# Joining the low bits of double-precision weights: a ScalarE copy for each chunk, and the engines' orders exchanged

## The chip, the core and the metric

The kernel runs on one core of one Trainium2 chip. The metric is the device time in microseconds (us) of one execution; of several executions the median is given. The engines are TensorE (PE in the rows; PEld are its weight loads), VectorE (DVE), ScalarE (ACT), GpSimd (POOL) and SyncE (SP), and the DMA queues are fed by SP, ACT and POOL.

## What is computed

Attention with a window of 32 positions and 32 global tokens for 8 batches and 8 heads, followed by a dense layer pair with a Mish-like activation. Cut to what matters:

```python
s_g  = scale * q_g @ concat(k_g, k_l).T;  out_g = softmax(s_g) @ v_all
s_ll = where(|i - j| <= 32, scale * q_l @ k_l.T, -1e9)
out_l = softmax(concat(scale * q_l @ k_g.T, s_ll)) @ concat(v_g, v_l)
x = concat(out_g, out_l)            # 8 x 544 tokens, 512 wide
h = x @ w_in                        # 512 x 2048
g = h * tanh(log1p(exp(h)))
out = g @ w_out                     # 2048 x 512
```

The attention inputs are float32. `w_in` and `w_out` arrive as float64, 8 MB each, so the kernel reads each weight as two 32-bit words and makes a float32 of them before it can use it.

## The kernel before

**Weights.** The two matrices are cut into 32 chunks of 512 KB, sixteen for each (`k` from 0 to 15 and from 16 to 31). A chunk is 128 partitions of 512 weights. `w_load` brings it into a raw buffer; chunks 0 to 4 are issued from ScalarE's queue, the others from GpSimd's, and GpSimd waits until the buffer is free. From chunk 21 on a load also waits for the statistic of the first matrix (`gate`). Three VectorE operations make float32 of it: `w_bits` (line 630) shifts the high word left by 3; the first of `w_sum` (line 637) joins sign and top exponent bit of the high word, the second (line 639) joins the low word shifted right by 29, which is its three top bits. Then `w_stat` (line 660) sums squares of a chunk by four small matmuls on TensorE, `w_norm` (lines 671 to 680, 546, 547) makes one scale for each matrix, with a reduction over the partitions on GpSimd between, and `w_split` (lines 537, 709, 710, 530, 715) writes the scaled weights as a high and a low float16 half into `W`. Where several engines can do a copy (`[(ACT, ...), (DVE, ...)]`), the planner picks one.

**Attention.** Units of one batch, one pair of heads and one of four tiles of 128 rows. For each: `scores` (line 895, TensorE), `row_max` (line 921, VectorE), `expo` (line 930, ScalarE), then in the first batch `p_cross` (transposes by TensorE, lines 971 and 985, with copies at line 537), later `p_hi`, `p_lo` and a DMA transpose; `pv` (line 1020, TensorE), `x_norm` (lines 1028 to 1030, VectorE) and `x_cross` (lines 996, 1004, 530, 532). `b_max` (lines 744 to 750) and `b_scale` (line 755 and on) find a scale for the values of each batch, `v_hi` and `v_lo` (lines 537, 830, 831, 530) split the values, and `v_move` copies pieces of them by small DMAs into the tile `vc`, which `pv` needs.

**Dense layers.** The tokens run in 17 blocks of 256. `m1_mm` (line 1173) is the first layer's matmul, `m2_mm` (line 1437) the second's; later blocks use sums of blocks (lines 1342 and 1532). The first block needs all four pairs of heads of the first batch and the split first matrix.

**Order.** Each operation is added as a task with its engine, a cost and its dependencies, numbered in the order of the calls of `add`. The planner (`Plan.run`) orders tasks by due times and modelled costs; then a list written by hand, `MOVES`, moves single tasks: `91 P 271` puts task 91 on TensorE (P; V is VectorE, A ScalarE, G GpSimd, S SyncE) right after task 271. Each engine runs its tasks in that fixed order and waits at each for what it needs. A buffer's next load waits for the last reader of the old content.

Of the kernel before, what the change touches and what calls it, by code (L numbers as in the profile page):

```python
# [73 lines left out]

MOVES = [(int(n), e, int(m)) for n, e, m in (x.split() for x in """91 P 271, 92 P 91, 93 P 92, 307 P 95, 284 P 275, 154 P 313, 350 P 154, 318 P 159, 164 P 330, 169 P 422, 174 P 343, 175 P 348, 176 P 358, 177 P 378, 178 P 392, 389 P 397, 398 P 389,
461 P 398, 179 P 421, 180 P 453, 454 P 180, 181 P 454, 450 P 474, 182 P 450, 475 P 182, 510 P 475, 183 P 510, 185 P 468, 557 P 555, 513 P 556, 526 P 558, 573 P 565, 566 P 573, 559
P 594, 664 P 642, 562 P 664, 580 P 562, 665 P 580, 680 P 665, 681 P 680, 703 P 622, 704 P 703, 625 P 629, 645 P 634, 666 P 645, 672 P 651, 652 P 672, 673 P 669, 705 P 673, 745 P
684, 747 P 745, 715 P 690, 716 P 708, 731 P 746, 732 P 748, 757 P 754, 769 P 757, 758 P 769, 818 P 783, 808 P 800, 35 V 18, 36 V 19, 37 V 20, 38 V 22, 232 V 39, 233 V 46, 43 V 233,
47 V 43, 44 V 47, 261 V 50, 262 V 54, 58 V 262, 56 V 62, 282 V 67, 283 V 71, 291 V 283, 296 V 291, 76 V 296, 267 V 81, 72 V 267, 73 V 83, 78 V 87, 292 V 88, 115 V 292, 111 V 115,
112 V 268, 274 V 297, 107 V 327, 101 V 107, 108 V 309, 103 V 322, 298 V 103, 104 V 298, 113 V 104, 380 V 113, 116 V 380, 328 V 116, 117 V 351, 123 V 119, 352 V 329, 127 V 366, 131  # L80
V 127, 373 V 424, 132 V 425, 133 V 135, 129 V 133, 374 V 129, 439 V 374, 381 V 136, 407 V 139, 137 V 407, 387 V 137, 403 V 387, 388 V 144, 370 V 388, 151 V 370, 371 V 151, 413 V
371, 372 V 413, 414 V 372, 418 V 414, 408 V 418, 384 V 408, 385 V 145, 148 V 448, 156 V 383, 157 V 431, 161 V 157, 412 V 161, 419 V 158, 449 V 419, 471 V 449, 149 V 471, 420 V 149,
396 V 466, 434 V 166, 459 V 401, 446 V 459, 163 V 171, 467 V 163, 168 V 172, 429 V 173, 472 V 429, 465 V 472, 529 V 465, 186 V 529, 480 V 186, 511 V 480, 534 V 188, 483 V 189, 457
V 483, 522 V 191, 512 V 478, 193 V 512, 524 V 193, 540 V 524, 535 V 540, 525 V 489, 195 V 525, 444 V 195, 906 V 444, 530 V 906, 536 V 531, 220 V 536, 907 V 220, 908 V 545, 230 V
908, 542 V 230, 260 V 550, 552 V 260, 520 V 560, 583 V 520, 584 V 583, 278 V 561, 910 V 578, 958 V 579, 587 V 585, 590 V 587, 591 V 588, 959 V 648, 649 V 959, 639 V 569, 620 V 639,
960 V 620, 961 V 960, 554 V 961, 786 V 554, 962 V 610, 624 V 962, 1001 V 643, 1002 V 644, 1003 V 1002, 575 V 1003, 1004 V 575, 687 V 1004, 1005 V 687, 1035 V 657, 621 V 1035, 1208
V 658, 688 V 1208, 1036 V 688, 667 V 678, 650 V 667, 631 V 650, 1037 V 631, 632 V 1037, 1209 V 632, 661 V 1209, 636 V 661, 668 V 636, 784 V 682, 637 V 683, 696 V 785, 697 V 810,
728 V 697, 729 V 706, 812 V 729, 654 V 707, 655 V 723, 700 V 655, 675 V 700, 813 V 1039, 676 V 813, 737 V 1062, 815 V 772, 738 V 815, 850 V 773, 1063 V 850, 730 V 1063, 693 V 1064,
694 V 752, 741 V 694, 718 V 741, 719 V 753, 1066 V 767, 768 V 1066, 776 V 1123, 821 V 776, 805 V 1124, 822 V 805, 806 V 1125, 779 V 734, 760 V 735, 761 V 790, 744 V 816, 1127 V
744, 1146 V 1127, 826 V 817, 1147 V 826, 823 V 1147, 787 V 823, 834 V 787, 797 V 834, 1148 V 797, 798 V 876, 802 V 798, 837 V 802, 803 V 864, 844 V 843, 235 A 226, 294 A 286, 295 A  # L90
294, 105 A 304, 317 A 105, 316 A 314, 312 A 316, 325 A 312, 335 A 331, 326 A 335, 355 A 340, 369 A 337, 342 A 438, 345 A 342, 440 A 344, 402 A 440, 360 A 347, 357 A 360, 359 A 349,
416 A 377, 379 A 416, 417 A 382, 451 A 417, 445 A 399, 395 A 445, 400 A 433, 462 A 400, 458 A 462, 427 A 458, 452 A 427, 469 A 452, 428 A 479, 463 A 428, 470 A 464, 477 A 456, 521
A 477, 482 A 521, 518 A 190, 192 A 443, 538 A 192, 539 A 538, 514 A 194, 219 A 514, 515 A 219, 527 A 515, 541 A 544, 528 A 229, 570 A 528, 519 A 259, 551 A 519, 277 A 551, 909 A
563, 279 A 564, 581 A 279, 567 A 582, 568 A 567, 711 A 609, 646 A 626, 656 A 627, 677 A 647, 713 A 677, 630 A 713, 635 A 630, 1038 A 660, 695 A 685, 720 A 686, 849 A 762, 692 A
849, 717 A 692, 740 A 717, 775 A 770, 804 A 771, 733 A 804, 836 A 833, 481 S 436, 523 S 485, 543 S 547, 640 S 593, 712 S 640, 659 S 749, 679 S 659, 714 S 679, 739 S 702, 764 S 739,
807 S 777""".split(","))]
# [1862 lines left out]
```

## Time and profile before

| | |
|---|---|
| median of 3 runs | 873.93 us (872.58 to 873.93) |
| the profiled execution's own time | 873.65 us |
| its span on the core | 871.9 us |
| TensorE busy | 840.7 us, 96% |
| VectorE busy | 747.9 us, 86% |
| ScalarE busy | 645.9 us, 74% |
| GpSimd busy | 169.4 us, 19% |
| mean DMA rate | 127 GB/s; 365, 372 and 358 in the first three of 40 slices |

The span is the time from the first to the last instruction of the program; what lies around it is 1.75 us here. A busy share is an average over the whole span, so the stages have to be looked at one by one. A row of a timeline gives start, time, engine, line, operation, what it writes and reads, how many were merged, and in square brackets the idle time of the engine ahead of it with what ended it.

### The profile page before, as it was taken

The numbers are of one execution on the slowest core, as the hardware profiler recorded it, in microseconds if no ns is written. First come the engines' busy times: TensorE is split into PE (matmuls) and PEld (weight loads), VectorE is DVE, ScalarE is ACT, GpSimd is POOL, SyncE is SP. The second block draws the span as 40 slices with busy tenths as digits, with TensorE's granted clock in tenths as the row PEclk, the third lists the DMA queues.
The fourth block names the chain that finished last, engine by engine and source line by source line (L and its number), as shares of the span: only waits on it lengthen the run. The fifth ranks groups of instructions, "written<-read, shape, count | busy, mean of one in ns | idle before, by whom it ended". The sixth has DMA issues, their size and how long they took to land.

```text
span 871.9 us, 24740 instructions
## 1 busy us (share of the span) xinstructions
PE 840.7 (96%) x9792; PEld 620.8 (71%) x9792; DVE 747.9 (86%) x1989; ACT 645.9 (74%) x1389; POOL 169.4 (19%) x324
## 2 busy tenths in 40 slices
PE   2789999999999999999999999999999999999997
PEld 1458667766675867876777776777777777689996
DVE  6999999668897798999879987998789999986675
ACT  2588988677698778989888877899888755464542
POOL 6220341033026103402330133112311000000000
PEclk9899999999999999999999999999999999999999
DMA  9994476375897976859676775475657541000000
GB/s 365 372 358 92 120 153 115 60 145 101 180 216 124 194 136 131 150 107 183 126 121 104 170 131 101 89 165 121 122 116 118 89 77 38 1 27 14 14 27 25
DMA packets 206885, 111.07 MB, mean 127 GB/s; under 512 B 186992, under 2 KB 191280, under 8 KB 205744
## 3 DMA queue, kind: packets, MB, share of 16 engines
q1 hardware_dynamic: 193952, 86.23, 48.9%
q0 software_dynamic: 11952, 20.37, 8.0%
q10 hardware_dynamic: 864, 2.88, 0.9%
q8 instruction: 77, 1.26, 0.6%
q14 instruction: 40, 0.33, 0.1%
HBM read 49.04 MB, written 8.91 MB: 66 GB/s over the span
## 4 chain that ended last, share of the span: by engine, by line
PE 89%; DVE 6%; DMA 2%; ACT 1%; issue 0%; POOL 0%; DVEq 0%; ACTq 0%
PE o L1437 33%; PE h L1342 25%; PE h L1173 11%; PE s L895 5%; PE U L1020 5%; PE o L1532 5%; PE gu L1124 1%; PE g L1058 1%; DVE W L637 1%; DMA raw<-in_w 1%; DVE W L639 1%; DVE W L630 1%; DMA W<-in_w 1%; DMA pt<-ph 1%; PE hx L1532 1%; DVE vmx L744 1%
## 5 line engine op out<-in xcount | busy, mean ns | idle before, releaser
L1437 PE MATMUL o<-W,G 128*128 128x512 f16 x1344 | 313.2, 379 | 0.0
L1437 PEld LDWEIGHTS <-G 128*128 128x128 f16 x1344 | 124.9, 98 | 128.5 <-issue 2.6
L1342 PEld LDWEIGHTS <-W 128*128 128x128 f16 x2880 | 166.0, 98 | 9.6 <-issue 0.2
L930 ACT ACTIVATE P<-P,nm 128x192 f32<-128x192 f32 (+1 forms) x256 | 117.8, 461 | 38.8 <-DVE nm L921 38.2
L1173 PE MATMUL h<-xh,W 128*128 128x256 f16 x640 | 114.4, 273 | 0.0
L1173 PEld LDWEIGHTS <-W 128*128 128x128 f16 x960 | 91.1, 98 | 16.7 <-issue 3.0
L1342 PE MATMUL h<-xh,W 128*128 128x128 f16 x1056 | 97.0, 219 | 0.0
L1342 PE MATMUL h<-xl,W 128*128 128x128 f16 x528 | 91.1, 219 | 0.0
L1173 PE MATMUL h<-xl,W 128*128 128x256 f16 x320 | 87.2, 272 | 0.0
L1342 PE MATMUL h<-raw,W 128*128 128x128 f16 x1152 | 73.2, 219 | 0.0
L854 POOL DMA_DIRECT2D vc<-vf x81 | 41.3, 512 | 155.6 <-DVE vf L835 110.3
L1020 PEld LDWEIGHTS <-pt 128*128 128x128 f16 (+1 forms) x1424 | 56.1, 98 | 18.9 <-issue 7.7
L895 PE MATMUL s<-qk 64*128 64x224 f16 (+3 forms) x640 | 56.2, 301 | 7.3 <-DMA qk<-in_qk 6.4
L921 DVE CUSTOM_DVE_ANT_0 P<-s,consts,sq 128x192 f32<-128x192 f32 (+1 forms) x128 | 53.0, 429 | 10.3 <-PE s L895 10.3
L537 ACT ACTIVATE ph<-P 128x384 f16<-128x384 f32 (+1 forms) x112 | 58.7, 538 | 3.3 <-DMA pt<-ph 2.6
L854 POOL DMA_DIRECT2D vgg<-vgf x84 | 44.3, 531 | 85.0 <-issue 47.9
L921 DVE CUSTOM_DVE_ANT_0 P<-s,consts 128x192 f32<-128x192 f32 (+1 forms) x128 | 45.5, 369 | 9.0 <-PE s L895 4.4
L1020 PE MATMUL U<-vc,pt 96*128 96x64 f16 (+1 forms) x656 | 52.3, 193 | 0.0
L1020 PE MATMUL U<-vf,pt 128*128 128x64 f16 x720 | 50.7, 194 | 0.7 <-DMA pt<-ph 0.7
L930 ACT ACTIVATION_READ_ACCUMULATOR P<-P,nm 128x1 f32 x256 | 48.1, 188 | 0.0
L530 ACT COPY EE<-h 128x512 f32<-128x512 f32 x47 | 27.2, 579 | 23.4 <-PE h L1342 16.2
L949 DVE SCALAR_TENSOR_TENSOR ph<-P,ph 128x256 f16<-128x256 f32 x112 | 38.5, 353 | 4.1 <-ACT ph L537 3.5
(281 smaller groups left out, 1750.8 us busy)
## 6 DMA issues: line engine op xcount, KB each, us to landing
qk<-in_qk SPq DMA_DIRECT2D x32, 704.0 KB, 5.2
out<-ob SPq DMA_DIRECT2D x33, 256.0 KB, 2.7
vraw<-in_vm SPq DMA_DIRECT2D x8, 1024.0 KB, 5.9
W<-in_w POOLq DMA_DIRECT2D x14, 512.0 KB, 7.5
raw<-in_w POOLq DMA_DIRECT2D x7, 512.0 KB, 7.3
G<-in_w POOLq DMA_DIRECT2D x6, 512.0 KB, 6.8
W<-in_w ACTq DMA_DIRECT2D x5, 512.0 KB, 10.6
pt<-ph SPq DMA_TRANSPOSE x120, 3.6
```

The costliest lines, as they stand in the source:

```text
L530: A.copy(dst, src)
L537: A.activation(out=dst, in_=src, func=AF.Copy, scale=c)
L854: stream(POOL, dma(kib), lambda: G.dma_start(dst(), src()), 512, r=[r], w=[w], new=new, table="dma")
L895: T.matmul(X[s[h]][:, cols(u)], part(b, hp, i)[r, u * 128:(u + 1) * 128], part(b, hp, j)[r, KO + OWN[u]:KO + OWN[u] + WIDTH[u]], start=n = ...
L921: pl.add(DVE, (134 if b >= QF else 77) + 1.03 * w, lambda: V.tensor_tensor_reduce(out=half(P, h, w), in0=X[s][:, cols(t)], in1=mask[:, m0: ...
L930: pl.add(ACT, 460, lambda: A.activation(out=half(P, h, w), in_=half(P, h, w), func=AF.Exp, bias=X[nm], scale=-1.0, accum_out=X[sums][:, t, ...
L949: pl.add(DVE, dve(2 * (z - a)), lambda a=a, z=z, q=q, o=o: V.scalar_tensor_tensor(X[ph][:, q, :, a + o:z + o], p_src(X[P], t)[:, :, a:z], ...
L1020: T.matmul(X[u][:, t, h, :], X[pt][:k, p * 4 + (c * 2 + h if turned(b, t) else h * 2 + c), :], X[vx][:k, t, vl, h * 64:(h + 1) * 64], star ...
L1173: T.matmul(X[h][:, f * TB:(f + 1) * TB], wh(i, wl)[:, off:off + 128], X[x][:, d, o:o + TB], start=(n == 0), stop=(n == 11))
L1342: T.matmul(X[h][:, c:c + 128], form(J + jj, wl)[:, off:off + 128], x(l, d), start=(p in (1, 2, 5) and c == 0 and n == 0), stop=(n == 5), s ...
L1437: T.matmul(X[o], gp(g, blk, i)[:, f, t * 128:(t + 1) * 128], wh(8 + i, wl)[:, f * 512:(f + 1) * 512], start=(turn == 0 and n == 0), stop=( ...
L1532: T.matmul(X[o][:, cols], a_form(a, jj, f), b_form(w, jj, f), start=(fresh and n == 0), stop=(n == 11), skip_group_check=True)
```

## The change

Where a chunk is in `BY_ACT` (all 32 are), `w_sum` adds a ScalarE task and one VectorE task in place of two VectorE tasks. `w_bits` stays ahead of them. The ScalarE task reads the upper halfword of each low word as an unsigned integer, divides it by 256, adds 4336 + 2^-9 and writes it as bf16 into the lower halfword of the high word: rounding to eight bits leaves the three top bits of the low word in the three lowest bits of that halfword. The VectorE task then takes sign, top exponent bit and those three bits from the high word by one mask and joins them. There are as many tasks as before, so the numbers in `MOVES` mean the same steps, but the list is another one: 387 entries in place of 344. The name `VMAX` is replaced by `VSQ`, which is empty, so that the branches that ask for it stay unused, and one lambda becomes a named function.

```diff
-VMAX = 99
+VSQ = ()
+BY_ACT = range(32)
...
-MOVES = [(int(n), e, int(m)) for n, e, m in (x.split() for x in """91 P 271, 92 P 91, 93 P 92, 307 P 95, ...
+MOVES = [(int(n), e, int(m)) for n, e, m in (x.split() for x in """84 P 237, 89 P 239, 90 P 89, 91 P 90, ...
...
+        if k in BY_ACT:
+
+            def w_low():
+                halves = raw(k).bitcast(U16).rearrange("p (f w) -> p f w", w=4)
+                A.activation(out=halves[:, :, 2].bitcast(BF16), in_=halves[:, :, 1], func=AF.Copy, scale=2.0 ** -8, bias=4336 + 2.0 ** -9)
+            pl.add(ACT, act(512), w_low, r=key, w=[rawkey(k)])
+
+            def w_join():
+                V.scalar_tensor_tensor(f(), word(k, 1), -0x3FFFFFF9, f(), ALU.bitwise_and, ALU.bitwise_or)
+            pl.add(DVE, 610, w_join, r=[rawkey(k)], w=key)
+            return
         pl.add(DVE, 610, lambda: V.scalar_tensor_tensor(f(), word(k, 1), -0x40000000, f(), ALU.bitwise_and, ALU.bitwise_or),
                r=[rawkey(k)], w=key)
         pl.add(DVE, 610, lambda: V.scalar_tensor_tensor(f(), word(k, 0), 29, f(), ALU.logical_shift_right, ALU.bitwise_or),
```

The entries of the new list that put copies of the start-up on VectorE which ran on ScalarE before (the list is otherwise left out; the steps are in the order of the entries):

```
23 V 22 (b_split)   201 V 42, 210 V 233, 241 V 40 (v_hi)   240 V 48, 288 V 274, 302 V 298, 331 V 127 (p_cross)
317 V 113, 319 V 384, 342 V 139, 364 V 414 (w_split)   402 V 129 (p_hi)   377 V 364, 379 V 158 (x_cross)
```

## Rows read from the trace of the kernel before

**Rows 1.** The page's 40 equal slices, busy tenths: TensorE, DMA engines.

```profile
PE   2789999999999999999999999999999999999997
...
DMA  9994476375897976859676775475657541000000
```

**Rows 2.** Windows by stage: length; busy us (instructions) by engine; clock, DMA, GB/s.

```profile
core 0: us, PE busy (x) PEld busy (x) DVE busy (x) ACT busy (x) POOL busy (x), PEclk, DMA share, GB/s
...
20.00:31.00 11.00, 10.23 (x50) 5.53 (x50) 10.83 (x31) 8.70 (x23) 3.03 (x5) 1.00 1.03 397
31.00:42.00 11.00, 6.46 (x75) 5.27 (x76) 10.95 (x29) 3.69 (x15) 3.31 (x6) 0.78 1.02 360
42.00:48.70 6.70, 5.64 (x65) 4.50 (x63) 6.43 (x25) 4.30 (x15) 3.23 (x7) 0.85 0.92 307
48.70:70.64 21.94, 20.29 (x153) 11.98 (x152) 21.87 (x66) 19.84 (x55) 2.40 (x5) 1.00 0.94 325
70.64:110.00 39.36, 39.36 (x405) 30.09 (x403) 38.76 (x92) 36.58 (x66) 8.92 (x18) 1.00 0.42 100
110.00:800.00 690.00, 689.28 (x8219) 500.20 (x8218) 599.55 (x1637) 538.34 (x1158) 134.74 (x260) 1.00 0.61 117
```

**Rows 3.** Windows of line 637 alone: length, VectorE's busy us (instructions), clock, DMA.

```profile
6.60:20.00 13.40, 2.65 (x4) 1.00 1.03 416
20.00:42.00 22.00, 7.95 (x12) 0.89 1.02 378
42.00:48.70 6.70, 1.37 (x2) 0.85 0.92 307
48.70:70.64 21.94, 5.40 (x8) 1.00 0.94 325
```

**Rows 4.** The chain that ended last: start, us on the chain, what.

```profile
16.63 1.20 DVE W L637 x2
```

**Rows 5.** Timeline of TensorE, 19 to 40 us.

```profile
19.16 0.61 PE L660 MATMUL ws<-W 128*128 128x128 bf16 x4 [6.67 <-DVE W L639]
19.70 1.76 PE L895 MATMUL s<-qk 64*128 64x192 f32 x8
...
30.88 0.97 PE L895 MATMUL s<-qk 64*128 64x192 f32 x8
...
39.81 0.61 PE L660 MATMUL ws<-W 128*128 128x128 bf16 x4 [3.34 <-DVE W L639]
```

**Rows 6.** ScalarE's groups by form: count, busy us and mean ns, idle before.

```profile
L530 ACT CAST xs<-x 128x512 f16<-128x512 f32 x24 | 14.8, 615 | 4.5 <-DVE x L1030 4.0
...
L537 ACT ACTIVATE G<-EE,c 128x512 f16<-128x512 f32 x17 | 12.1, 718 | 0.2
```

**Rows 7.** Line 630 by itself: min/median/max ns, first and last start.

```profile
L630 DVE TENSOR_SCALAR W<-W x19: 411/422/1029, 6.6 to 67.9; 128x512 int32<-128x512 int32 x19
```

**Rows 8.** Timeline of VectorE, 40 to 48 us.

```profile
40.28 1.28 DVE L639 SCALAR_TENSOR_TENSOR W<-W 128x512 int32<-128x512 int32 x2
...
44.99 0.28 DVE L671 CUSTOM_DVE_ANT_0 wd<-ws,consts 128x128 f32<-128x128 f32 x1
...
47.88 0.16 DVE L547 RECIPROCAL sw<-iw 128x1 f32<-128x1 f32 x1
```

**Rows 9.** Timeline of TensorE's weight loads: the first of the dense layer.

```profile
70.64 1.25 PEld L1173 LDWEIGHTS <-W 128*128 128x128 f16 x12
```

**Rows 10.** The sixteenth chunk: its issue (timeline), and its us to landing (DMAs).

```profile
31.35 0.53 POOL L612 DMA_DIRECT2D W<-in_w  x1 [2.43 <-DVE W L639]
...
W<-in_w POOLq DMA_DIRECT2D x1, 512.0 KB, 4.5
```

**Rows 11.** Windows by stage around 40 us, columns as in rows 2.

```profile
36.00:40.00 4.00, 0.61 (x7) 0.42 (x7) 4.00 (x10) 0.00 (x0) 0.00 (x0) 0.64 1.02 366
40.00:44.00 4.00, 3.90 (x45) 3.63 (x44) 3.85 (x11) 0.57 (x2) 0.00 (x0) 0.50 1.03 319
```

**Rows 12.** The tile `vc`, 30 to 50 us: its DMAs' time to landing.

```profile
DMA to landing us min/median/max: 3.8/5.9/8.4
```

More of the change, by code (lines that the diff above doesn't have):

```diff
@@ L16 @@
 BF16 = mybir.dt.bfloat16
+U16 = mybir.dt.uint16
 AF = mybir.ActivationFunctionType
@@ L95 @@
-849, 717 A 692, 740 A 717, 775 A 770, 804 A 771, 733 A 804, 836 A 833, 481 S 436, 523 S 485, 543 S 547, 640 S 593, 712 S 640, 659 S 749, 679 S 659, 714 S 679, 739 S 702, 764 S 739,
-807 S 777""".split(","))]
+MOVES = [(int(n), e, int(m)) for n, e, m in (x.split() for x in """84 P 237, 89 P 239, 90 P 89, 91 P 90, 281 P 242, 271 P 269, 92 P 271, 93 P 92, 307 P 97, 263 P 234, 100 P 275, 284 P 299, 154 P 301, 310 P 303, 305 P 310, 350 P 313, 330 P 320, 334
+P 159, 422 P 386, 174 P 356, 175 P 174, 353 P 175, 358 P 353, 176 P 363, 447 P 376, 177 P 378, 389 P 177, 397 P 392, 421 P 461, 178 P 421, 426 P 178, 453 P 426, 179 P 453, 454 P
@@ new lines @@
+50, 240 V 48, 262 V 56, 266 V 262, 62 V 266, 282 V 66, 283 V 282, 60 V 283, 267 V 71, 296 V 267, 291 V 76, 292 V 81, 268 V 88, 297 V 268, 274 V 107, 288 V 274, 308 V 288, 309 V
+101, 322 V 109, 327 V 103, 302 V 298, 328 V 323, 104 V 328, 119 V 104, 113 V 119, 317 V 113, 123 V 351, 370 V 352, 384 V 370, 319 V 384, 371 V 117, 121 V 365, 331 V 127, 125 V 331,
+406 V 424, 131 V 425, 381 V 131, 139 V 381, 342 V 139, 373 V 342, 402 V 129, 439 V 402, 374 V 439, 135 V 374, 156 V 137, 385 V 156, 387 V 385, 407 V 387, 147 V 407, 403 V 147, 388
@@ new lines @@
+V 403, 413 V 388, 405 V 413, 372 V 151, 414 V 372, 364 V 414, 377 V 364, 158 V 377, 379 V 158, 418 V 379, 161 V 418, 419 V 161, 141 V 419, 383 V 141, 430 V 383, 412 V 153, 458 V
+412, 149 V 163, 420 V 448, 431 V 449, 396 V 431, 466 V 396, 459 V 466, 463 V 459, 467 V 463, 433 V 467, 166 V 433, 445 V 166, 434 V 445, 462 V 434, 446 V 462, 479 V 446, 171 V 471,
+480 V 171, 511 V 472, 529 V 511, 429 V 168, 400 V 429, 408 V 173, 401 V 408, 534 V 401, 464 V 534, 473 V 464, 465 V 186, 483 V 189, 457 V 483, 478 V 191, 512 V 478, 522 V 512, 193
@@ new lines @@
+V 522, 524 V 193, 535 V 524, 530 V 535, 540 V 530, 525 V 540, 906 V 195, 531 V 500, 536 V 531, 907 V 220, 545 V 907, 908 V 545, 230 V 908, 520 V 560, 583 V 520, 584 V 583, 561 V
+584, 910 V 578, 579 V 910, 585 V 958, 590 V 587, 591 V 588, 959 V 648, 280 V 649, 620 V 280, 569 V 620, 639 V 569, 960 V 639, 961 V 960, 786 V 554, 623 V 786, 962 V 610, 1001 V
+643, 1002 V 644, 1003 V 1002, 575 V 1003, 1004 V 575, 1005 V 687, 1035 V 657, 621 V 1035, 1208 V 658, 688 V 1208, 1036 V 688, 667 V 678, 650 V 667, 1209 V 650, 1037 V 631, 661 V
@@ new lines @@
+632, 636 V 661, 784 V 682, 683 V 784, 785 V 637, 696 V 785, 810 V 696, 811 V 697, 729 V 706, 812 V 729, 654 V 707, 655 V 723, 700 V 655, 675 V 700, 1039 V 724, 813 V 1039, 676 V
+813, 1062 V 676, 737 V 1062, 815 V 772, 738 V 815, 850 V 763, 1063 V 850, 730 V 1063, 1064 V 730, 693 V 1064, 694 V 752, 741 V 694, 1066 V 767, 1123 V 768, 776 V 1123, 1124 V 821,
+805 V 1124, 1125 V 822, 806 V 1125, 734 V 774, 735 V 779, 761 V 790, 744 V 816, 1127 V 744, 1146 V 1127, 826 V 817, 1147 V 826, 823 V 1147, 787 V 823, 834 V 787, 797 V 834, 1148 V
@@ new lines @@
+797, 798 V 876, 802 V 798, 837 V 802, 24 A 36, 250 A 203, 14 A 250, 47 A 226, 51 A 238, 228 A 51, 243 A 228, 63 A 55, 236 A 264, 270 A 59, 286 A 77, 252 A 286, 295 A 87, 276 A 295,
+294 A 108, 311 A 300, 116 A 311, 304 A 116, 112 A 304, 105 A 306, 312 A 105, 120 A 124, 354 A 120, 333 A 340, 128 A 333, 355 A 132, 344 A 345, 440 A 344, 347 A 440, 360 A 136, 357
+A 360, 349 A 357, 359 A 349, 362 A 157, 390 A 362, 382 A 391, 411 A 417, 162 A 411, 394 A 162, 395 A 394, 399 A 395, 470 A 167, 469 A 470, 427 A 469, 428 A 172, 521 A 428, 455 A
@@ L99 @@
+S 750, 547 S 546, 592 S 589, 593 S 592, 712 S 640, 659 S 749, 679 S 659, 714 S 679, 739 S 702, 764 S 739, 1189 S 764""".split(","))]
 class Plan:
@@ L733, in b_max @@
         m = ("vmx", b)
-        if b >= VMAX:
+        if b in VSQ:
             src = lambda: X["vraw", b][:, hp].rearrange("p a c -> p (a c)") if hp < HP else X["vgraw", b]
@@ L758, in go @@
             q, s = X[p], X[sv]
-            if b >= VMAX:
+            if b in VSQ:
                 V.tensor_scalar(q, q, TINY * TINY, None, ALU.max)
@@ L1876, in attn_mish_kernel, with warm_up @@
     V.memset(pmax, 0.0)
-    pl.add(POOL, 600, lambda: G.partition_all_reduce(warm, pmax, 128, RED.max))
+    def warm_up():
+        G.partition_all_reduce(warm, pmax, 128, RED.max)
+    pl.add(POOL, 600, warm_up)
     for i, x in enumerate(ORDER.split()):
```

26 lines of the change are left out of this document (6 added, 20 removed).

## The prediction

> **What bounds the kernel now.** I read the page's forty slices first, for TensorE and the DMA [rows 1], then the windows by stage [rows 2], then who waited for whom around the weights. In the slices the reader should see that TensorE is full from the fourth slice on, and that the DMA engines are full in the first three. The windows say where the line runs: from 70.64 us, where TensorE loads the first weights of the dense layer [rows 9], it is busy 39.36 us of 39.36, and then 689.28 of 690 [rows 2]. So the end of the kernel is the start of that stage plus a constant, as long as TensorE stays fed: what the change is worth is how much sooner 70.64 us comes.
>
> Before that point the windows show two full resources. VectorE is busy 10.83 of 11, 10.95 of 11, and 21.87 of 21.94 us, and the DMA share is 1.03, 1.02, 0.92 and 0.94, while ScalarE has 7.3 us of 11 free in the third row, and TensorE 4.5 us [rows 2]. TensorE's waits name VectorE's last weight operation, line 639: 6.67 us before the matmuls at 19.16, 3.34 us before those at 39.81 [rows 5]. So the start-up is a VectorE queue beside a DMA queue.
>
> The stage splits at the scale of the first weight matrix, which needs all sixteen of its chunks: the last two of them are joined at 40.28 to 41.56 us, the statistic is read at 44.99 and the scale is there at 47.88 to 48.04 [rows 8]. From then to 70.64 TensorE is busy 20.29 of 21.94 us [rows 2]: this last part is nearly full on TensorE too, and a relief of VectorE can shorten it only by the 1.65 us that are idle, or by work that moves ahead of it.
>
> **What the change removes.** Each chunk costs VectorE three operations now and two afterwards. The removed one, line 637, takes 0.60 us from start to start where two follow each other (1.20 for two) [rows 4]. It runs 4 times in 6.6 to 20 us, 12 times up to 42, 2 times up to 48.7 and 8 times up to 70.64 [rows 3], of 32 in all: 26 before the dense layer, so 26 x 0.60 = 15.6 us leave VectorE's queue there. The last operation of a chunk stays one of the same kind with the same two tensors (a new mask, an `or`), so I cost it at the old 0.60.
>
> **What it adds.** One ScalarE copy per chunk, 512 halfwords with a step of 8 bytes on both sides, to bf16, with the scale and bias as constants. No row shows this form. Nearest are a contiguous cast of 512 elements between two tiles, 0.615 us, and one with a scale from a tile, 0.718 us [rows 6]; below, nothing makes it cheaper than the first, and above I have only the row with the dearer operand. I take 0.61, as it is nearest in kind (no operand from a tile). The copy waits for line 630 of its chunk, and the join waits for the copy: one chunk by itself takes 0.42 (line 630) [rows 7] + 0.61 + 0.68 (1.28 for two joins less 0.60) [rows 8] = 1.71 us, no shorter than now; only throughput is gained. Behind a waiting copy stand ScalarE's exponentials and evacuations, for which TensorE's transposes wait; behind a waiting join stand the row maxima.
>
> Counting the calls of `add` gives the numbers in the exchange list. Among the tasks that it now puts on VectorE are fifteen copies of the start-up that ran on ScalarE: three `v_hi`, four `p_cross`, four copies of `w_split`, the first `b_split`, one `p_hi`, two of `x_cross`. At 0.34 us for each 512 columns or each short copy (a 0.42 us operation less its overlap) [rows 7], and two such pieces where the data come from PSUM or are 1024 wide, these are about 2.0 us before 42 us, 1.4 us up to 48.7, and 4.4 us in the last part. ScalarE is rid of about 4.8 us in that last part (0.615 for 512 columns, about twice that for 1024) [rows 6]. These are estimates from those rows.
>
> **Loads.** A chunk's buffer comes free with its join, as before, and GpSimd's queue issues the next load then. The DMA is full to 42 us [rows 2], so earlier issues do not bring chunks sooner: the sixteenth chunk was issued at 31.35 and landed 4.5 us later, at 35.85 [rows 10]. That is a floor.
>
> **The sum, stage by stage.** (a) To 20 us: of the path through the first value maxima, four operations of line 637 go, 2.4 us; the values land only just before, so I take 2. This shifts the next stage, and no more, since TensorE was waiting there.
>
> (b) 20 to 48.7 us: VectorE loses 12 x 0.60 = 7.2 and gains 2.0 us. With (a) its queue would finish the first matrix at 41.56 - 2 - 5.2 = 34.4 us, which is earlier than the load. So the floor decides: 35.85 + 1.71 = 37.6 us, 4.0 sooner than 41.56. From the last join to the scale there are now 6.5 us; the 3.1 us from the statistic to the scale stay, while the 3.4 us before it [rows 8] are TensorE catching up behind other matmuls. There TensorE first waits (0.61 us busy of the four from 36 us) and then runs on half its clock: 0.50 of it is granted from 40 to 44 us (1.2 of 2.4 GHz), where it is busy 3.90 us [rows 11]. What half the clock costs can be read from one row shape, eight score matmuls in 1.76 us at 19.70 and 0.97 us at 30.88 [rows 5]. If the wait goes, that fall goes too, and about 3.90/2 = 1.9 us come back. I take 2 of the 3.4. The scale is there 6.0 us sooner.
>
> (c) 48.7 to 70.64 us: VectorE 21.87 - 4.8 + 4.4 = 21.5 us, ScalarE 19.84 + 8 x 0.61 - 4.8 = 19.9, TensorE 20.29. All three stay near full; I take 0.5 us from the 1.65 that TensorE has idle.
>
> (d) After 70.64: six more of line 637 go, from a stage where TensorE does not wait. Nothing. The second matrix has to land sooner as well; the DMA share falls to 0.42 after 70.64 [rows 2], so its last load has room.
>
> So 6.0 + 0.5 = 6.5 us. The profiled execution took 873.65 us (its span of 871.9 and 1.75 around it), 0.28 below the median of 873.93 and inside the runs' spread. 873.65 - 6.5 = 867.15, forecast 867.2 us.
>
> **The rivals.** *TensorE packs better.* Work that needs no scale (scores, transposes, value products) fills the gaps of (b). The bound is the 2 us of (a) out of the 6.67 before 19.16 [rows 5], all of TensorE's idle time from 20 us, 0.77 + 4.54 + 1.06 + 1.65 [rows 2], and half of the cold 3.90: 12.0 us in all, 861.7. Against it: the value products need small copies that land 3.8 to 8.4 us after their issue in the full DMA [rows 12], and their buffers are few.
>
> *Part is given back.* The copies of the last part stay where ScalarE has 2.1 us idle, and its order is less good than I count: with half of the relieved 4.8 us lost, (c) grows by 2.4 - 0.5, and (b) stays: 6.0 - 1.9 = 4.1 us, 869.5 to 871.
>
> *Tied to the DMA.* If the small copies of rows 12 hold TensorE between 36 and 44 us, not the weights, the scale comes sooner but the attention of the first batch does not, and the dense layer needs both. Then about 1 us is left: 872.7. For it: DMA share 1.02 there. Against it: the wait that the trace names is line 639.
>
> *The copy is slow on ScalarE.* In (c) it decides from 8d - 4.8 - 2.1 = 6.5, d = 1.68 us. At three times the 0.60 us of the operation replaced, d = 1.8 us, (c) grows by 7.5 us: 1.0 us slower, 874.7, no change within what can be measured. The rows speak against it, 0.615 and 0.718 for 512 elements. The Trainium skill's page "ScalarE: Activation LUTs", under "Rules for kernel authors", speaks against the change as a rule: plain arithmetic belongs on VectorE, which it puts at up to about three times faster per element (in bf16, with one source). By that rule the sum would be this rival's 874.7 in place of 867.2. No run here shows it so far; the replaced operation reads two tensors, and its row is no faster than the ScalarE row.
>
> *Slower.* ScalarE works in order, and its copy now depends on a load by way of line 630. Chunks of the second matrix land one after another at 325 GB/s [rows 2], 512 KB in 1.6 us. If ScalarE stands for one such landing in front of each of the 8 copies of (c), they cost 8 x (0.61 + 1.6) = 17.7 us less 4.8 and 2.1: 10.8 us against the 6.5 gained, 4.3 us slower, 878. It decides from a stand of 1.07 us each. Against it: VectorE runs behind the landings now, so chunks lie ready.
>
> **How the numbers follow.** The forecast (865 to 869) 0.48; better packing 0.13; part given back 0.17; tied to the DMA 0.07; a slow copy 0.03; slower by ScalarE's standing 0.12. 0.2% is 1.75 us, about what a measurement of this kernel can tell from no change. Faster: 0.48 + 0.13 + 0.17 = 0.78; the same: 0.07 + 0.03 = 0.10; slower 0.12. The range goes from 861, just past the packing bound, to 873.0, past the DMA case; it leaves out the slower case, the slow copy and a little at the low end.
>
> **What would show it.** Right: the first dense matmul at about 64 us; the copy at 0.6 to 0.7 us; TensorE's waits for weights in 30 to 42 us gone, and no half clock near 40 us; VectorE with gaps before 42 us. Wrong: ScalarE idle before its copies, released by line 630; the first dense matmul no sooner than 69 us; a new gap of TensorE after it, in front of the second layer, if the second matrix's scale comes no sooner; or a copy of over 1 us.

## The result and the profile after

The changed kernel takes 884.7 us (median of four, 883.81 to 885.23) where the kernel before, run beside it, takes 873.25 (872.32 to 873.93): ratio 1.0131, 95% interval 1.0113 to 1.0148. It is 1.3% slower; the forecast had it 0.8% faster. Its profiled execution took 884.48 us, with a span of 882.7.

The stage windows of after, with the bounds and columns of [rows 2]:

```profile
20.00:31.00 11.00, 8.29 (x47) 4.25 (x46) 6.11 (x17) 9.57 (x18) 2.13 (x4) 1.00 1.03 397
31.00:42.00 11.00, 5.86 (x37) 4.13 (x36) 7.47 (x25) 9.47 (x21) 3.44 (x6) 0.67 0.94 323
42.00:48.70 6.70, 5.62 (x68) 4.56 (x67) 4.77 (x16) 4.53 (x8) 0.51 (x2) 0.77 0.89 300
48.70:70.64 21.94, 17.25 (x133) 9.75 (x130) 18.71 (x58) 21.03 (x51) 5.29 (x10) 1.00 0.82 305
70.64:110.00 39.36, 34.83 (x379) 27.70 (x377) 34.80 (x97) 34.53 (x57) 3.33 (x5) 1.00 0.40 88
```

VectorE (third figure) has the room that it was to get: 7.47 instead of 10.95 us busy from 31 to 42. ScalarE (fourth) has taken its place: 9.47 instead of 3.69 there, and 21.03 of 21.94 in the last part. TensorE is 3.0 us less busy in that part [rows 2]. In the row behind 70.64 it is 4.5 us less busy, but there the dense layer runs only from 79.49.

The new copy by itself (the view of line 645: min/median/max ns, first and last start, form):

```profile
L645 ACT ACTIVATE W<-W x19: 1323/1354/1430, 7.9 to 78.9; 128x512 bf16<-128x512 uint16 x19
```

Two of the waits up to 110 us (total, times, longest):

```profile
PEld L675 <- DVE W L649: 10.8, 6, 4.7
DVE W L649 <- ACT W L645: 10.8, 12, 2.4
```

1.35 us, where the prediction took 0.61. The joins wait for it 12 times, and TensorE's statistic for the joins. The last join of the first matrix, its statistic and the scale (VectorE's timeline), and the dense layer's first weight load (TensorE's), answering to [rows 8, 9]:

```profile
44.79 0.69 DVE L649 SCALAR_TENSOR_TENSOR W<-W 128x512 int32<-128x512 int32 x1 [0.45 <-ACT W L645]
...
47.80 0.28 DVE L686 CUSTOM_DVE_ANT_0 wd<-ws,consts 128x128 f32<-128x128 f32 x1
...
52.31 0.16 DVE L551 RECIPROCAL sw<-iw 128x1 f32<-128x1 f32 x1
```

```profile
79.49 0.56 PEld L1188 LDWEIGHTS <-W 128*128 128x128 f16 x6
```

The scale comes 4.4 us later than before (47.88), the dense layer 8.9 later (70.64), and the span is 10.8 longer. The chain that ended last (the work followed back from the last instruction, at each step to what released it) has the copy again and again from 52 us on: 9.6 us of the 27 up to the dense layer (start, us, what):

```profile
52.16 1.35 ACT W L645
...
56.31 2.41 ACT raw L645 x2
...
64.94 1.24 ACT G L645
...
69.75 1.27 ACT G L645
...
75.65 1.41 ACT raw L645
```

### The profile page after: what moved, and what is told of

The parts are those of the page before. It is cut to its first block, busy times and chain, and to the rows that moved or that the text cites. A ratio compares the mean times of both kernels' runs of the same rounds, so it can differ in the third digit from the quotient of the medians.

```text
span 882.7 us, 24752 instructions
## 1 busy us (share of the span) xinstructions
PE 843.2 (96%) x9792; PEld 620.9 (70%) x9792; DVE 741.8 (84%) x1985; ACT 667.5 (76%) x1393; POOL 169.3 (19%) x324
## 4 chain that ended last, share of the span: by engine, by line
PE 81%; DVE 5%; ACT 4%; issue 3%; DMA 1%; POOL 0%; DVEq 0%; SPq 0%; ACTq 0%; POOLq 0%
PE o L1452 31%; PE h L1357 25%; PE h L1188 8%; PE o L1547 4%; PE U L1035 4%; PE s L910 4%; DMA pt<-ph 1%; PE gu L1139 1%; PE g L1073 1%; ACT W L645 1%; ACT pt L541 1%; PE hx L1547 1%; DVE W L730 1%; ACT G L645 1%; ACT raw L645 0%
## 5 line engine op out<-in xcount | busy, mean ns | idle before, releaser
L869 POOL DMA_DIRECT2D vgg<-vgf x84 | 44.4, 533 | 85.9 <-issue 48.8
L541 ACT ACTIVATE ph<-P 128x384 f16<-128x384 f32 (+1 forms) x108 | 56.5, 538 | 2.9 <-DMA pt<-ph 2.1
L967 DVE SCALAR_TENSOR_TENSOR ph<-P,ph 128x448 f16<-128x448 f32 x64 | 39.3, 615 | 3.0 <-ACT ph L541 2.3
```

Of the source, the lines that this page charges most:

```text
L541: A.activation(out=dst, in_=src, func=AF.Copy, scale=c)
L869: stream(POOL, dma(kib), lambda: G.dma_start(dst(), src()), 512, r=[r], w=[w], new=new, table="dma")
L967: pl.add(DVE, dve(n), lambda: V.scalar_tensor_tensor(p_part(X[ph], t, 1), p_src(X[P], t), PSC, p_part(X[ph], t, 0), ALU.mult, ALU.subtract ...
```

## The experiments

Theory A: the copy's price on ScalarE is the loss. B: the added waits are. C: the exchanged orders are. Each group of runs stood beside runs of the kernel before (873.25 to 874.6 us), so the ratios are what to compare. "Dense" is the first dense matmul in the profiled execution; 70.69 us before, 79.51 after.

| run | us | ratio, interval | copy, us | scale, us | dense, us |
|---|---|---|---|---|---|
| e1_contig | 871.57 | 0.9972, 0.9963 to 0.9981 | 0.63 | 46.09 | 69.03 |
| e2_orders | 888.78 | 1.0174, 1.0157 to 1.0191 | none | 51.88 | 79.60 |
| e3_copies | 895.23 | 1.0247, 1.0231 to 1.0262 | 1.35 | 56.74 | 86.84 |
| e4_word | 871.87 | 0.9972, 0.9963 to 0.9982 | 0.68 | 44.71 | 68.18 |
| e5_onecol | 873.2 | 0.9989, 0.998 to 0.9999 | none | 47.93 | 70.33 |
| e6_subset | 875.66 | 1.0022, 1.0012 to 1.0031 | 1.36, nine | 49.70 | 72.49 |
| e7_contig_old | 877.96 | 1.005, 1.0035 to 1.0065 | 0.63 | 47.64 | 73.07 |
| e8_onecol_copy | 870.65 | 0.9954, 0.9939 to 0.9969 | 0.20 | 46.36 | 68.18 |
| e9_twice | 884.01 | 1.0106, 1.0088 to 1.0124 | 2 x 0.67 | 49.52 | 76.76 |
| e10_slow2 | 879.1 | 1.0052, 1.0037 to 1.0067 | 1.38 in half | 47.22 | 74.44 |
| e11_stat_first | 871.97 | 0.9978, 0.9968 to 0.9987 | 0.20 | 41.29 | 69.04 |
| e12_before_stat | 874.83 | 1.0009, 0.9999 to 1.0018 | none | 46.80 | 73.16 |
| e13_stat_quarter | 870.15 | 0.9955, 0.994 to 0.997 | 0.20 | 46.78 | 68.27 |
| e14_before_quarter | 873.58 | 0.9994, 0.9984 to 1.0003 | none | 47.67 | 70.52 |
| e15_both | 871.55 | 0.997, 0.9958 to 0.9983 | none | 48.27 | 70.37 |

**e1_contig: the copy without gaps.** All orders as in after, and both added waits: the copy's for line 634 (630 before) and the join's for the copy.

```diff
-halves = raw(k).bitcast(U16).rearrange("p (f w) -> p f w", w=4)
-A.activation(out=halves[:, :, 2].bitcast(BF16), in_=halves[:, :, 1], ...)
+halves = raw(k).bitcast(U16)
+A.activation(out=halves[:, 512:1024].bitcast(BF16), in_=halves[:, :512], ...)
```

> The changed kernel with its orders, but the 32 ScalarE copies read and write contiguous halfwords (512 of them, step 2 bytes on both sides) in place of every fourth; it leaves out the signs and the low bits of the weights. Theory A (the copy's own price, 1.34 us where 0.61 was taken, is what loses the time): the copy falls to 0.6 us, the first dense matmul comes at about 64 us, and the kernel takes 865 to 870 us. Rival B (the added waits between VectorE and ScalarE and the exchanged orders lose it, whatever the copy costs): 878 us or more.

871.57 us, just above theory A's range: with the price that the forecast took, the change is 0.28% faster. So the price carries the sign of the result. ScalarE still stood before its copies for line 634 here (11.9 us in 6 times, more than the 7.8 in 4 of after), so B falls. But 0.28% is 2.4 us, not the 6.5 of the sum: a second step of the forecast is wrong too.

**e2_orders and e3_copies: the operations and the orders apart.** e2 runs the three VectorE operations of before in after's queue orders, e3 the operations of after in before's orders.

```diff
-    lanes[names[e]].insert(lanes[names[e]].index(m) + 1 if m >= 0 else 0, n)
+    lanes[e].append(int(x))
+    self.on[int(x)] = e
```

> The old three VectorE operations in the changed kernel's orders, with line 637's operation put directly ahead of the join; so the exchange of orders, and the copies moved to VectorE, without the ScalarE copy. Theory A: VectorE carries 26 x 0.60 = 15.6 us of joins again and about 7.8 us of moved copies on top before the dense layer, so it is slower than before by some of these 7.8 us, 876 to 882 us. Rival C (the orders alone carry the loss): 884 us or more.

> The changed kernel's operations in the old orders: line 637 taken out of VectorE's queue, the ScalarE copy put into ScalarE's queue at the time at which the plan had line 637. Theory A: 26 copies at about 1.15 us from start to start are 30 us on ScalarE before the dense layer, of which it has about 23 idle, and none of its copies has moved to VectorE: slower than before by 8 to 20 us, 881 to 893 us. Rival C (the new orders carry the loss): about 873 us or less.

Both are slower than after: 888.78 and 895.23 us. In e2 VectorE keeps line 637 and has fifteen more copies, 10.8 of 11 us busy in both windows from 20 to 42. That is C's range, but e1 has the same orders and is faster than before: they are bad only for a VectorE that keeps line 637. In e3 joins wait 21.3 us for copies up to 110 us (14 times), and it came out above its range. Neither half of the change works by itself.

**probe1 and probe2: the copy by itself.** Programs with nothing but copies and shifts of 512 elements; probe2 has each form on a line of its own.

```diff
+A.activation(out=view(outs[i], BF16, 4, 512), in_=view(src, U16, 4, 512), func=AF.Copy, ...)
+A.activation(out=view(outs[i], BF16, 1, 512), in_=view(src, U16, 4, 512), func=AF.Copy, ...)
```

> The copy's forms by themselves, four of each in a row, 512 elements from one tile to others; it computes nothing of the reference. Theory A1 (the step of 8 bytes costs, on either side): the copy with the step on one side alone takes 0.6 to 1.3 us, contiguous halfwords 0.61 us, float32 with a step of two words as much as halfwords with a step of four. Rival A2 (the unsigned 16-bit type costs): contiguous unsigned halfwords take 1.3 us as well, bf16 with the step 0.61. VectorE's shift of the same halfwords, meant to take the copy's place: 0.42 us as line 630 if the step doesn't matter there, 0.68 us otherwise.

> A program of its own, none of the kernel's work: ScalarE's copy of 512 elements for 128 partitions, each form on a line of its own, four times: read with steps of 2, 4 and 8 bytes, written with steps of 2, 4 and 8 bytes, in 2 or 4 bytes, also with 256 elements, and VectorE's 16-bit shift with the same steps. In the kernel the copy that reads and writes 2 bytes with a step of 8 took 1.34 us, the one that writes 4 bytes with a step of 8 took 0.68, the one without gaps 0.63. Theory W (only 2-byte writes with gaps cost): the forms that write 2 bytes with a step of 8 take 1.3 to 1.4 us however they read and with 256 elements about 0.75, all others 0.6 to 0.7. Theory R (the price comes from a read and a write of 2 bytes in the same 8 bytes): 1.3 us only where the copy is in place, 0.6 to 0.7 where it reads without gaps.

In probe1 several forms shared a line; it left open whether the read or the write costs. Rival A2 falls there: read as bf16 with the same steps, the copy took 1.35 us as well. In probe2 (groups by line and form: busy us, mean ns) the lines are: 39 as in the change (2 bytes read and written with a step of 8 bytes), 40 the same read, written without gaps, 41 read without gaps, written with a step of 8, 44 read without gaps, written with a step of 4, 45 the read of the change, written as 4 bytes with a step of 8, 48 and 49 4-byte numbers with a step of 16 in the write and in the read, 56 VectorE's shift with a step of 8 on both sides, 59 without gaps:

```profile
L39 ACT ACTIVATE dst<-src 128x512 bf16<-128x512 uint16 x4 | 5.3, 1336 | 6.1 <-DVE dst L31 6.1
...
L41 ACT ACTIVATE dst<-src 128x512 bf16<-128x512 uint16 x4 | 4.7, 1370 | 0.0
...
L49 ACT ACTIVATE dst<-src 128x512 f32<-128x512 f32 x4 | 4.0, 1083 | 0.0
L48 ACT ACTIVATE dst<-src 128x512 f32<-128x512 f32 x4 | 3.8, 1094 | 0.0
L56 DVE TENSOR_SCALAR dst<-src 128x512 uint16<-128x512 uint16 x4 | 3.0, 739 | 41.5 <-ACT dst L54 41.5
L44 ACT ACTIVATE dst<-src 128x512 bf16<-128x512 uint16 x4 | 2.6, 750 | 0.0
...
L40 ACT ACTIVATE dst<-src 128x512 bf16<-128x512 uint16 x4 | 2.3, 651 | 0.0
L45 ACT ACTIVATE dst<-src 128x512 f32<-128x512 uint16 x4 | 2.2, 636 | 0.0
...
L59 DVE TENSOR_SCALAR dst<-src 128x512 uint16<-128x512 uint16 x4 | 0.9, 294 | 0.0
```

Theory W holds: the read costs nothing (40), the write of 2 bytes with a step of 8 costs 1.34 to 1.37 us however it reads (39, 41), and the same step with 4 bytes 0.64 (45).

**e4_word: the same step, four bytes wide.**

```diff
-A.activation(out=halves[:, :, 2].bitcast(BF16), in_=halves[:, :, 1], ...)
+A.activation(out=raw(k).bitcast(F32).rearrange("p (f w) -> p f w", w=2)[:, :, 0], in_=halves[:, :, 1], ...)
-V.scalar_tensor_tensor(f(), word(k, 1), -0x3FFFFFF9, f(), ...)
+V.scalar_tensor_tensor(f(), word(k, 1), -0x40000000, f(), ...)
```

> The changed kernel with one word of the copy changed: it writes the same 512 numbers with the same step of 8 bytes, but as 4 bytes, over the low word that it has just read (the join then takes the sign alone, so the three low bits of the weights are left out). Instructions, orders, waits and reads are those of the changed kernel. Theory A with W (2-byte writes with gaps are what costs, and the copy's price is the whole loss): copy 0.63 to 0.68 us, time 870.5 to 873, as with the copy without gaps (871.57). Theory R (the read with gaps costs): copy over 1 us, time 880 to 885.

As A with W had it in the copy's price and in the time. But, against what was expected, the waits are not those of the changed kernel: this copy writes the low word alone, which neither line 634 nor the new join reads, and in the trace both added waits are gone. What ended ScalarE's idle time before the copy, and who waited for the copy (us, times), in e1 and then in e4:

```profile
  DVE W L634: 11.9, 6
...
  DVE W L649: 2.9, 4
```

```profile
  DMA W<-in_w: 7.1, 4
...
  POOL W L616: 3.4, 2
```

The ninth join of e4 starts at 27.36 us, its copy at 27.87. The same holds wherever the copy writes 4 bytes: in e8, e9, e11, e13 and the first matrix of e10.

Line 645, and the windows from 31 to 42 and of the last part:

```profile
L645 ACT ACTIVATE W<-W x19: 646/682/735, 6.9 to 67.0; 128x512 f32<-128x512 uint16 x19
```

```profile
31.00:42.00 11.00, 7.70 (x101) 6.03 (x102) 9.98 (x35) 8.83 (x27) 2.43 (x4) 1.00 1.04 366
...
48.70:70.64 21.94, 19.41 (x154) 11.48 (x154) 21.87 (x67) 19.54 (x48) 2.12 (x4) 1.00 0.90 303
```

VectorE is full again in the last part and ScalarE is not. The granted clock is 1.00 (2.4 GHz) from 31 to 42 us, where TensorE is busy 7.70 us; in after it was 0.67, with TensorE busy 5.86. After's ratio lies 1.6% above e4's. Price and waits both differ there; e1, which keeps the waits, has the same ratio as e4, so at the cheap price the waits cost nothing that can be measured.

**e9_twice and e10_slow2: how the price acts, and where.** e9 issues the cheap copy twice; e10 has the cheap one for the first weight matrix and the dear one for the second.

```diff
+A.activation(out=raw(k).bitcast(F32).rearrange("p (f w) -> p f w", w=2)[:, :, 0], in_=halves[:, :, 1], ...)
```

```diff
+dst = raw(k).bitcast(F32).rearrange("p (f w) -> p f w", w=2)[:, :, 0] if k < 16 else halves[:, :, 2].bitcast(BF16)
```

> As e4_word, with the cheap copy (4-byte write) issued twice in a row, 2 x 0.55 us, so that ScalarE is held about as long as by one copy of the changed kernel (1.34), by writes that are not 2 bytes wide. The low bits are left out. Theory A (ScalarE's time for the copy is the loss, however it comes about): 880 to 885, as the changed kernel (884.7). If 2-byte writes with gaps do more than hold ScalarE (slow other engines or transfers): 873 to 877.

> The changed kernel in its orders, with the cheap copy (4-byte write, low bits left out) for the first weight matrix's 16 chunks and the copy of the changed kernel (2-byte write, 1.34 us) for the second matrix's 16. It tells in which part the 12.9 us between e4_word (871.87) and the changed kernel (884.7) arise. The first matrix's scale stood at 44.71 us in e4_word and at 52.31 in the changed kernel. If the loss is made before that scale: 874 to 877. If it is made by the second matrix's copies, which stand among the dense layer's own copies: 880 to 884.

e9 is as slow as after (the intervals overlap): it is ScalarE's time that costs, not anything else that such writes might do. ScalarE's window from 31 to 42 us (fourth figure, 10.81 of 11):

```profile
31.00:42.00 11.00, 6.77 (x75) 5.66 (x76) 7.03 (x23) 10.81 (x28) 3.21 (x6) 0.84 1.04 359
```

And no join waits for a copy in e9: the sixteenth starts at 37.68 us, its copies at 41.75 and 42.42. So price and waits are told apart by four runs: with a cheap copy 0.9972 with the waits (e1) and 0.9972 without (e4), with a dear one 1.0131 with them (after) and 1.0106 without (e9). The price is the loss; the waits add at most a little to it. e10 lies between the two ranges given for it: 0.8% over e4, of the 1.6% to after. So half of the loss comes from the second matrix's copies, which stand among the work ahead of the dense layer (they have the waits again, joins 1.7 us in 3 times); in e10 the scale is late by 2.5 us against e4 and the dense layer by 6.3.

**e5_onecol and e8_onecol_copy: a copy that is free.** e5 is the kernel before without the third operation's time, in before's orders; e8 is e4 with the copy on one column, in after's orders.

```diff
-V.scalar_tensor_tensor(f(), word(k, 0), 29, f(), ALU.logical_shift_right, ALU.bitwise_or)
+V.scalar_tensor_tensor(one(f()), one(word(k, 0)), 29, one(f()), ALU.logical_shift_right, ALU.bitwise_or)
```

> The kernel before with line 639 (the join of the low bits) on one column instead of 512: the third operation stays in its place with its waits, at some 0.07 us instead of 0.60; the three low bits of the weights are left out. ScalarE and all orders are those of before. It is what VectorE's relief is worth with no copy anywhere. Theory V (the forecast's step: VectorE's 0.60 us per chunk holds the scale, and the landings only from 35.85 us on): scale 5 to 7 us sooner, time 866 to 868.5. Theory L (VectorE would only wait for landings and for TensorE instead): scale 1 to 3 us sooner, 870.5 to 872.5.

> As e4_word (the changed kernel in its orders, the copy written as 4 bytes, the low bits left out), with the copy on one column instead of 512, so at some 0.22 us instead of 0.68: it is the change with a copy that is as good as free. Theory A (the copy's price alone stood between the forecast and the result, and the forecast's sum is right for a cheap copy): 866 to 868.5. Theory L (from a price of 0.65 us on, landings and the order of the queues hold the scale; the forecast's 6.5 us of gain were never there): 870 to 872.5, first dense matmul at 67.5 to 69 us.

e5 takes about half a microsecond off VectorE for every chunk and gains 0.1%; e8 gains 0.46%, about 4.0 us. In these orders the 6.5 us were not there at any price; theory L was the better one, though e5 came out above its range, with the scale no sooner than before (47.93). VectorE's timeline in e5 shows one place where the room goes (in brackets: idle before, what ended it):

```profile
37.58 0.08 DVE L922 DVE_READ_ACCUMULATOR2_ANT nm<- 128x1 f32 x1
41.83 0.43 DVE L630 TENSOR_SCALAR W<-raw 128x512 int32<-128x512 int32 x1 [4.16 <-DMA raw<-in_w]
...
45.03 0.28 DVE L672 CUSTOM_DVE_ANT_0 wd<-ws,consts 128x128 f32<-128x128 f32 x1
```

The sixteenth chunk is joined before 38 us, but the next operation in VectorE's queue is line 630 of a chunk that has not landed; the statistic, further back, comes at 45.03, as before. The kernel before has that landing on its own chain, on the way to the scale, and the forecast did not count it:

```profile
33.11 8.79 DMA raw<-in_w
...
42.27 0.42 DVE W L630
...
45.08 0.20 DVE wd L671
```

**e6_subset and e7_contig_old: copies in the old orders.** e6 has the true copy for nine chunks, e7 the copy without gaps for all.

```diff
-BY_ACT = range(32)
+BY_ACT = (0, 1, 2, 3, 12, 13, 14, 15, 17)
```

> The kernel before in its own orders, computing everything; for nine chunks alone (0 to 3, 12 to 15 and 17, whose joins fall where ScalarE stood idle, at 13 to 20 and 36 to 42 us) line 637 is taken off VectorE and the copy, at its 1.34 us, stands on ScalarE in its place. Theory A (the price matters where ScalarE is full): 9 x 0.6 = 5.4 us off VectorE, copies in idle time, 870 to 872.5. Theory L (VectorE would only wait instead, for landings or for the copy itself, which stands between two of its operations): 872.5 to 875.

> As e3_copies (the operations of the changed kernel in the orders of the kernel before, line 637's tasks off VectorE and the copies on ScalarE at their planned times), but with the copy without gaps (0.62 us; signs and low bits of the weights are left out, as in e1_contig). Against e1_contig (871.57) it tells what the new orders are worth at the cheap price; against e3_copies (895.23) what the price is worth in the old orders. Theory A (price): 870 to 876. If the old orders rather than the price made e3_copies slow: over 882.

Both lose, e6 by 0.2%, just above theory L's range. e6 put the copies where ScalarE stood idle, and VectorE waited for them (`W L758 <- ACT W L754` 6.3 us in 5 times); the loads behind those joins moved less, 332 GB/s from 31 to 42 us where before moved 360 [rows 2]. Idle time on an engine is not room for a step that stands between two steps of another. e7, just above its range, is 0.8% slower than e1 with the same copy: that much the new orders are worth at the cheap price. And it is 2% faster than e3, which is the price in the old orders.

**e11_stat_first and e12_before_stat: the scale alone sooner.** Queue orders of e11; e12 is the like in before's queues.

```diff
 TensorE, from the scores of the fourth pair on:
-pv, pv, w_stat 13, w_stat 14, x_cross, p_cross, x_cross, w_stat 15
+w_stat 13, w_stat 14, w_stat 15, pv, pv, x_cross, p_cross, x_cross
```

> As e8_onecol_copy (the changed kernel with the copy on one column, low bits left out; 870.65), with the first matrix's scale moved ahead in the queues and nothing else: on TensorE the statistic's matmuls of the last three chunks ahead of the matmuls that wait for a transfer of vc at 38.66, on VectorE line 686 right behind the sixteenth join and lines 692 to 695 and 551 ahead of two operations each. The scale should be there at 41 to 43 us instead of 46.36. Theory S (the scale sets the dense layer's start, as the forecast had it): first dense matmul 3 to 5 us sooner than 68.18, time 866 to 868. Theory D (from the scale on VectorE's own work, 21.73 busy of 21.94 us in e8, sets it, and the scale is only one task among it): first dense matmul at 67.5 to 69 us, time 869.5 to 872.

> The kernel before, computing everything, with the same move in its own queues: the statistic's matmuls of the last three chunks ahead of the matmuls of line 1020 that stand before them, line 671 on VectorE some 2 us sooner, lines 677 to 680 and 547 sooner likewise. The scale should be there at 45 to 46.5 us instead of 47.88. Theory S: first dense matmul 1.5 to 3 us sooner than 70.64, time 871 to 872.5. Theory D: 873.5 to 875.

e11's scale (VectorE's timeline) and first dense weight load (TensorE's):

```profile
41.29 0.16 DVE L660 RECIPROCAL sw<-iw 128x1 f32<-128x1 f32 x1
```

```profile
69.01 0.67 PEld L1297 LDWEIGHTS <-W 128*128 128x128 f16 x7
```

The scale is 5.1 us sooner than in e8 and the dense layer no sooner. Theory S falls: the dense layer's start doesn't follow the scale. In e12 the scale came 1.1 us sooner, a little later than expected, and the dense layer 2.5 us later; the time, 0.1% up, can't be told from no change.

**e13_stat_quarter, e14_before_quarter, e15_both: what sets the start.** TensorE is relieved in e8 (e13), in before (e14), and in e5 (e15).

```diff
-for c in range(4):
+for c in range(4 if k < 16 else 1):
```

> As e8_onecol_copy (the changed kernel's orders, copy on one column, low bits left out; 870.65), with TensorE's statistic of the second weight matrix on one quarter of the columns (one matmul of four for its 16 chunks; the other three quarters are left out of that statistic). Nothing is taken from VectorE, ScalarE or the transfers. The four take 2.58 us in 48.7 to 70.64 us and 2.83 after, so 1.9 and 2.1 us of TensorE's time go. Theory P (TensorE's own queue sets the dense layer's start): first dense matmul 1.5 to 2.5 us sooner than 68.18, time 866 to 867.5. Theory D (VectorE, 21.73 busy of 21.94 us there, sets it): first dense matmul at 67.5 to 68.7 us, and only what TensorE is rid of afterwards comes off: 868 to 869.5.

> The kernel before with the same cut: TensorE's statistic of the second weight matrix on one quarter of the columns, all else as it was. The four take 2.93 us in 48.7 to 70.64 us and 3.21 after, so 2.2 and 2.4 us of TensorE's time go. Theory P: first dense matmul 1.7 to 2.7 us sooner than 70.64, time 4 to 5 us shorter, 869.5 to 871. Theory D: first dense matmul at 70 to 71 us, 2 to 3 us shorter, 871.5 to 872.5.

> The kernel before with both cuts: line 639 on one column (e5_onecol) and TensorE's statistic of the second weight matrix on one quarter of the columns (e14_before_quarter), so that the second matrix's scale leaves out three quarters and all weights leave out their three low bits. Alone the cuts brought 0.8 and 0.6 us. Theory of two bounds (VectorE and TensorE stand within a microsecond of each other before the dense layer, so that each relief alone is lost to the other): first dense matmul 1.5 to 2.5 us sooner than 70.64, time 3 to 5 us under the kernel before, more than the two alone together. If the bound is a third (ScalarE, a landing, or the second scale): 1 to 2 us under it.

Neither e13 nor e14 moved the start (68.27, 70.52 us): theory P falls. They gained less than D gave them, too: what TensorE was rid of after the start did not come off either (in e13 it is busy 38.57 us from 70.64 to 110, in e8 all 39.36). The windows of the last part of e13, e5 and e15:

```profile
48.70:70.64 21.94, 19.67 (x147) 11.15 (x148) 21.87 (x66) 16.31 (x52) 2.12 (x4) 1.00 0.93 316
```

```profile
48.70:70.64 21.94, 20.54 (x163) 12.51 (x161) 19.24 (x71) 20.25 (x58) 2.45 (x5) 1.00 0.93 327
```

```profile
48.70:70.64 21.94, 19.95 (x145) 11.12 (x143) 19.26 (x71) 20.43 (x58) 2.62 (x5) 1.00 0.93 327
```

In e13 VectorE is full. In e5 VectorE has 2.7 us to spare, and from 61.86 us on the chain that ended last has left it for TensorE and ScalarE:

```profile
63.97 1.05 ACT W L537
65.02 0.54 ACT pt L537 x2
65.60 0.38 PE PT L986 x2
...
66.21 0.98 PE rest L710 x2
67.20 0.22 PE rest L711
```

In e15, with TensorE relieved as well, ScalarE is the busiest (20.43 us), the dense layer still starts at 70.37, and the 0.3% gained are made after it (second layer at 93.84 us, before 95.54). Its time lies between the two theories' ranges for it; the start itself speaks for the third bound, though ScalarE is not full there, and no run relieves it in these orders.

## Why the prediction was wrong, step by step

**The copy's price, 0.61 us.** This term decided the sign. It was read from copies without gaps [rows 6], and a contiguous copy did cost that (0.63 in e1); the form of the change costs 1.35. The prediction said that above it had only the row with the dearer operand, 0.718, and closed the range there. The spread was not covered: it reached a slow copy only as a rival with 0.03, whose decision point, 1.68 us, was worked out in (c) alone and after taking 4.8 and 2.1 us of room off.

**(b), ScalarE's load from 20 to 42 us.** The step counts VectorE's queue, the landings and TensorE's clock, and not ScalarE. With the cheap price ScalarE keeps free time: in e1, where the joins wait for the copies, it is busy 6.95 and 8.57 of 11 us in the two windows, and the sixteenth join ends at 39.84 us, where the sum had 37.6. At 1.35 us it is busy 9.57 and 9.47, and that join starts at 44.79. The scale is 6.2 us later than in e1. The join's wait is not needed for it: in e9 the sixteenth join is early, and the scale still comes at 49.52.

**(c), the last part.** From scale to dense layer e4 takes 23.47 us with 6.47 us of copies on ScalarE, which is busy 21.55; after takes 27.20 with 13.12 (e1: 22.94 with 5.95). The added 6.65 less the 1.92 that ScalarE had free makes 4.7; 3.7 were measured. The mechanism of the rival was right and its size not.

**(d), nothing after 70.64.** The span loses another 2 us beyond the start of the dense layer: of the 39.36 us from there TensorE is busy 37.62 in after, and all of them before [rows 2]. Its longest stand waits for ScalarE's activation function of the first layer (line 1234):

```profile
87.47 0.27 PE L1188 MATMUL h<-xh,W 128*128 128x256 f16 x1 [1.32 <-ACT EE L1234]
```

**The steps that the cheap price leaves wrong.** The floor of the loads was nearly right for the sixteenth chunk: its join was to end at 37.6 us and ends at 38.0 in e8 and 38.5 in e4, where it does not wait for the copy, and at 39.8 in e1. But it is not the floor of the scale: before's chain has a landing at 41.9 us on that way, and e5 stands for it. From the join to the scale the sum took 4.3 us; e8 needs 8.3, e4 and e1 6.3. In e8 TensorE waits 1.23 us for a small copy of `vc` and has a granted clock of 0.75 from 31 to 42 us, so the wait and the fall of the clock that were to go stayed; in e4 the clock stayed at 1.00, and it took 2 us more than the sum all the same. What half the clock costs can't be read from the two score rows that the prediction takes, either: a window of its own in the trace gives each a granted 1.00, and what made the first slow is not shown. Value products of one shape show it (TensorE's timeline before): groups of three start 0.16 us apart near 41 us, at a granted 0.50, and 0.09 apart from 44.4 us, at 1.00. And the step "the scale is there 6 us sooner, so the dense layer is" falls with e11, where the scale came 6.6 us sooner than before and the dense layer 1.65. The rival "tied to the DMA" named this (the dense layer needs the attention of the first batch as well) and gave 872.7; e1 and e4 measured 871.6 and 871.9. But in e11, whose chain to the scale holds no such copy, the dense layer comes no sooner, so what ties it looks rather like the work of the last part: VectorE 21.87, TensorE 20.29 and ScalarE 19.84 of 21.94 us [rows 2]. The prediction had read that all three are near full, and yet let a relief further ahead pass through the stage whole. e5, e13 and e15 fit with a bound that goes on to the next when one or two are relieved.

**The rival "slower".** Its mechanism, ScalarE standing for landings, was not it: e1 stood longer than after and was faster. The signs named as wrong were seen: a copy over 1 us, the dense layer after 69 us, ScalarE idle for line 634 (630 before), and a gap of TensorE ahead of the second layer, though for ScalarE and not for the second scale. The first was the cause.

The Trainium skill speaks of both sides of this. The Trainium skill's rule in "ScalarE: Activation LUTs" ("Rules for kernel authors"), plain arithmetic on VectorE, was right in its result here, though not by the rate: without gaps the copy took 0.63 us, about the 0.60 of the VectorE operation that it replaced. The Trainium skill's page "SBUF — State Buffer" ("Specifications (TRN2)") says that full bandwidth needs two accesses or more to each 16-byte line. Reads with a step of 8 bytes (0.65 us), 4-byte writes with it (0.64) and the loss with one access per line (1.08 and 1.09 at a step of 16) agree; by it the change's copy would take 0.64 too, and 1.34 was measured, so for 2-byte writes the measurement decides.

What stays open: which single wait sets the dense layer's start when the copy is cheap was not isolated. In the old orders neither an earlier scale (e12), VectorE (e5) nor TensorE (e14) alone moves it by more than 0.4 us to the better. In the new orders neither the scale (e11) nor TensorE (e13) does, nor ScalarE (e8 against e4, both at 68.18); there VectorE, busy 21.45 to 21.87 of 21.94 us in e8, e11 and e13, remains the nearest candidate, and no run takes work from it. No run that computes everything is faster than the kernel before; those that are leave out bits of the weights or a part of a statistic.

## What to carry to other kernels

Price an operation by a row of its own form, width and step of the write included; where no row has that form, the range must reach to what twice the nearest row would do to every stage in which the engine works, not only to the one looked at. Work moved from a full engine to one with free time is only gained while that engine keeps free time: count the new load stage by stage. Where three engines are near full in a stage, a relief ahead of it or of one of them passes through as a fraction; look at where the chain goes next before adding up.

## What the runs showed of the hardware

ScalarE's write of 2-byte numbers depends on the step: 512 of them for 128 partitions took 0.65 us without gaps, 0.75 with a step of 4 bytes and 1.34 to 1.37 with a step of 8 (probe2), while 4-byte numbers took 0.64 with a step of 8 and 1.09 with a step of 16. The read's step of 8 bytes cost nothing. VectorE's 16-bit shift took 0.29 us without gaps and 0.74 with a step of 8 bytes on both sides.
